# Routing of the early groups on VectorE, with small operands in PSUM

## The chip, the cores and the metric

The kernel runs on one core of one Trainium2 chip. The metric is the time of one execution in device microseconds (us). A core has a matrix engine (TensorE, PE in the profile), VectorE (DVE), ScalarE (ACT), GpSimd (POOL) and queues that issue DMA transfers (SyncE, SP). Each engine works through its own queue of instructions in order; semaphores hold an instruction until what it needs is there. SBUF is the on-chip memory, 128 partitions wide; PSUM is the smaller memory into which TensorE writes its products.

## The reference

Linear attention over 8 batches of 8 heads with 576 rows, then a mixture of 8 experts over the 4608 rows that come out of it. Each row goes to one expert only.

```python
def phi(x):
    proj = np.einsum('bhsd,df->bhsf', x, w_phi)
    proj = proj - np.max(np.abs(proj), axis=-1, keepdims=True)
    return np.concatenate([np.exp(proj), np.exp(-proj)], axis=-1)
q_p, k_p = (phi(q), phi(k))
kv = np.einsum('bhsf,bhsd->bhfd', k_p, v)
...
num = np.einsum('bhsf,bhfd->bhsd', q_p, kv)
...
logits = x @ w_gate
expert_idx = np.argmax(logits, axis=1)
logits_shift = logits - logits.max(-1, keepdims=True)
probs = np.exp(logits_shift)
probs /= probs.sum(-1, keepdims=True) + 1e-09
gate_w = probs[np.arange(N), expert_idx]
...
    h = np.maximum(xe @ w1[e], 0.0)
    ye = h @ w2[e]
    out[mask] = gate_w[mask, None] * ye
```

## The kernel before

**Two parts.** Up to about 424 us the attention runs; then the routed rows are gathered expert by expert, in blocks of 128, and go through the two products of their expert, mostly two blocks at a time. All products are made from pairs of rounded operands: a tile x is split into a high part (xh, kh, vh, wh: a copy in the rounded type, mostly on ScalarE) and the remainder (xl, kl, vl, wl: a subtraction, on VectorE or GpSimd), and three products take the place of one.

**Units.** The attention is worked in 16 units u = 0 to 15, about 24 us each: group g = u // 4 is two batches, and each of its four units is two heads. A unit projects its rows of k and q (`project`, L245 to 266: ps_proj on TensorE; mx, the row's maximum, and t, the subtraction, on VectorE), forms exponentials (e for k on ScalarE, then kh and kl; for q TensorE transposes t into pt and ScalarE makes qp), sums k against v into pk (L334), copies that to kvT (ScalarE, L351), unfolds it into pf and kf (L360, L370), and multiplies by qp into pn (L382). `normalize` (L404ff) divides (rec, xrow, lgc). lgc holds the logits of the group's rows, head by head. Rows of the result (xrow) are stored to DRAM for the gathers of the second part.

**Routing.** `route` (L590ff) is called once for each group. For groups 0 to 2 its steps are spread into the second, third and fourth unit of the next group, that is from u = 5, 9 and 13 on ("group 1", "2", "3" in the prediction are these three stretches, at about 130 to 156, 231 to 257 and 333 to 359 us): `spread` puts one step behind every sixth item of the unit. All 9 chunks of 128 rows are handled at once. The steps: lg (sum of the logits over the heads), lmax, the shift by it, cand (which expert has the maximum, as a number), choice (the smallest such), oh_b (one-hot, bf16), onehot (its float copy), gsum and base (running counts), some empty steps, prk (the rank of each row within its expert: nine products of oh_b on TensorE, all in one buffer), rks, rki (rank), rkb and rki (rank divided by 128, and the remainder), blk and rkr (their float copies), sel_p and sel_h (selection matrices by rkr, nine each, on VectorE and GpSimd), and the gates: ex on ScalarE, se (sum, plus 1e-9, reciprocal) and gt (the gate columns, stored to DRAM). Instructions named X in the code run on GpSimd for these groups and on VectorE for the last one. After the last early group `lead` (L734ff) finds the largest expert so far (lcand, ld, key, before), its rows (bl, b0, pl, gidx0) and gathers them early. The last group is routed at about 430 us in two parts, at the start of the expert part, and `place` (L552ff) lays out the blocks (first, paired, start, spot).

**What sets the order.** The products on TensorE follow a written order (`half` and `ordered`: sums into pk, unfolding and pn interleaved). Everything else is placed by a scheduler that goes by data and priorities; a block under `tc.high_priority(offset=200)` is taken earlier. Each engine then runs its list in the order found. PSUM buffers come from pools with two buffers for each tag: ps_pr for ps_proj, ps_tr for pt, ps_nm for pn, and ps_kv with the one tag "pk", which pk, pf, prk, pc, pl and pp share.

Of the kernel before, what the change touches and what calls it, by code (L numbers as in the profile page):

```python
# [19 lines left out]
P = 128  # L20
# [3 lines left out]
E = 8  # L24
# [4 lines left out]
NC = 9  # L29
# [9 lines left out]
NEARLY = (NG - 1) * NC  # L39
# [10 lines left out]
def tile_linear_attention_moe(  # L50
# [11 lines left out]
    nc = tc.nc  # L62
# [101 lines left out]
    blk = rt.tile([P, NTILE], F32, name="blk")  # L164
# [429 lines left out]
    def route(g, lgc, c0, n, final=None):  # L594
# [9 lines left out]
        def tile_of(name, shape, dtype=F32, **kw):  # L604
            r[name] = sg.tile(shape, dtype, name=name, **kw)[:, 0:n]
            return r[name]
# [20 lines left out]
        def first_top():  # L627
            V.tensor_reduce(choice[:, js], r["cand"], axis=AX.X, op=ALU.min)

        def one_hot():  # L630
            oh_b = tile_of("oh_b", [P, NC, E], BF16)
            V.tensor_tensor(
                oh_b,
                iota_em.unsqueeze(1).to_broadcast([P, n, E]),
                choice[:, js].unsqueeze(2).to_broadcast([P, n, E]),
                op=ALU.is_equal,
            )
            X.tensor_copy(onehot[:, js, :], oh_b)
            r["base_b"] = sg.tile([P, E], BF16, name="base_b")
            X.tensor_copy(r["base_b"], base)  # L640
# [9 lines left out]
        def sum_up():  # L650
            if not final:
                gsum = sg.tile([P, E], F32, name="gsum")
                V.tensor_reduce(gsum, onehot[:, js, :].rearrange("p c e -> p e c"), axis=AX.X, op=ALU.add)
                X.tensor_tensor(base, base, gsum, op=ALU.add)

        def count_ranks():
            oh_b, base_b = r["oh_b"], r["base_b"]
            prk = ps_kv.tile([P, n, E], F32, name="prk", tag="pk")
            T.matmul(prk, ltri, oh_b, start=True, stop=False)
            for c in range(n - 1):  # L660
                m = n - 1 - c
                T.matmul(
                    prk[:, c + 1 :, :], ones, oh_b[:, c : c + 1, :].to_broadcast([P, m, E]), start=False, stop=False
                )
            T.matmul(prk, ones, base_b.unsqueeze(1).to_broadcast([P, n, E]), start=False, stop=True)
            with tc.high_priority(offset=200 if final is None else 0):
                V.tensor_tensor(tile_of("rks", [P, NC, E]), prk, onehot[:, js, :], op=ALU.mult)

        def rank():
            with nc.allow_low_precision("ranks are integers"):  # L670
                V.tensor_reduce(tile_of("rki", [P, NC], I32), r["rks"], axis=AX.X, op=ALU.add)

        def rank_parts():
            rkb = tile_of("rkb", [P, NC], I32)
            V.tensor_single_scalar(rkb, r["rki"], 7, op=ALU.arith_shift_right)
            V.tensor_single_scalar(r["rki"], r["rki"], P - 1, op=ALU.bitwise_and)

        def rank_values():
            X.tensor_copy(blk[:, js], r["rkb"])
            X.tensor_copy(tile_of("rkr", [P, NC], bufs=2), r["rki"])  # L680

        def select_a(c):

# [15 lines left out]
            A.activation(tile_of("ex", [P, NC, E]), r["lg"], AF.Exp)  # L699

        def gate_sum():
            V.tensor_reduce(tile_of("se", [P, NC]), r["ex"], axis=AX.X, op=ALU.add)
            X.tensor_scalar_add(r["se"], r["se"], 1e-9)

        def gate_store():
            V.reciprocal(r["se"], r["se"])
# [1 line left out]
            X.tensor_copy(gt[:, 0:n], r["se"].unsqueeze(2).to_broadcast([P, n, XW - DM]))  # L708
            store_rows(g, gt, DM, XW - DM, c0, n)

        steps = [logits, top, shift, candidates, first_top, one_hot]
        selects = [lambda c=c: select(c) for c in range(n)]
        ranks = [rank, rank_parts, rank_values]
        gates = [gate, gate_sum, gate_store]
        if final is not None:

            def all_of(fs):
# [7 lines left out]
                *selects,  # L725
                all_of(gates),
            ]
        return steps + [sum_up] + PAUSE * [pause] + [count_ranks, pause] + ranks + selects + gates


    ON_ACT = (0, 2, 4, 6, 8)
# [2 lines left out]
    def lead():  # L734


        r = {}

        def pick():
            base_b = sg.tile([P, E], BF16, name="lbase_b")  # L740
            V.tensor_copy(base_b, base)
            r["base_b"] = base_b

        def pick_lead():
            pc = ps_kv.tile([P, E], F32, name="pc", tag="pk")
            T.matmul(pc, ones, r["base_b"], start=True, stop=True)
            top = sg.tile([P, 1], F32, name="top")
            V.tensor_reduce(top, pc, axis=AX.X, op=ALU.max)
            cand = sg.tile([P, E], F32, name="lcand")
            V.tensor_scalar(cand, pc, top, -float(E), op0=ALU.is_ge, op1=ALU.mult)  # L750
            V.tensor_tensor(cand, cand, iota_e, op=ALU.add)
            ld = sg.tile([P, 1], F32, name="ld")
            V.tensor_reduce(ld, cand, axis=AX.X, op=ALU.min)
            V.tensor_scalar_add(lead_e, ld[0:1], float(E))
            key = sg.tile([P, E], F32, name="key")
            V.tensor_scalar(key, iota_em, ld, -2.0 * E, op0=ALU.is_equal, op1=ALU.mult)
            V.tensor_tensor(key, key, iota_e, op=ALU.add)

            V.tensor_tensor(
                before,  # L760
                key.unsqueeze(2).to_broadcast([P, E, E]),
                key.unsqueeze(1).to_broadcast([P, E, E]),
                op=ALU.is_gt,
            )
            r["ld"] = ld

        def find():
            bl = sg.tile([P, NEARLY], F32, name="bl")
            V.tensor_scalar(bl, choice[:, 0:NEARLY], r["ld"], 64.0, op0=ALU.not_equal, op1=ALU.mult)
            V.tensor_tensor(bl, bl, blk[:, 0:NEARLY], op=ALU.add)  # L770
            b0 = sg.tile([P, NEARLY, NLEAD], BF16, name="b0")
            V.tensor_tensor(
                b0,
                iota_p[:, 0:NLEAD].unsqueeze(1).to_broadcast([P, NEARLY, NLEAD]),
                bl.unsqueeze(2).to_broadcast([P, NEARLY, NLEAD]),
                op=ALU.is_equal,
            )
# [470 lines left out]
```

## Time and profile before

| what | value |
|---|---|
| median of 3 runs | 932.68 us (931.11 to 932.99) |
| the profiled execution | 931.82 us |
| its span, first to last instruction | 929.9 us (1.92 around it) |
| mean granted TensorE clock | 0.99 |
| TensorE busy | 895.1 us, 96% of the span |
| VectorE busy | 589.4 us, 63% |
| ScalarE busy | 592.4 us, 64% |
| GpSimd busy | 496.6 us, 53% |

TensorE is busy nearly all the time and the other engines for little more than half of it. Such a share is a mean over stages, so the views by stretch and the list of TensorE's waits tell more than these numbers.

### The profile page before, as it was taken

What the parts mean: (1) busy time and instruction counts of PE and PEld (TensorE: products, weight loads), DVE (VectorE), ACT (ScalarE), POOL (GpSimd) and SP (SyncE); (2) the same over time, 40 slices, a digit from 0 to 9 for tenths busy, and PEclk for the clock granted to TensorE, in tenths of its full rate; (3) what the DMA queues carried; (4) which work ended last, traced back from release to release, by engine and by line L of the source; (5) the groups of instructions that cost most, each with busy time, mean ns of one, the idle gap of its engine ahead of it and who ended that gap; (6) DMA issues with size and microseconds to landing.
All of it is one profiled execution on the core that took longest, in us unless ns stands there. A gap on an engine that the chain in (4) does not pass through costs nothing. (4 is left out here: it accounts for less than half of the span.)

```text
span 929.9 us, 18409 instructions
## 1 busy us (share of the span) xinstructions
PE 895.1 (96%) x6831; PEld 837.6 (90%) x6831; DVE 589.4 (63%) x1015; ACT 592.4 (64%) x897; POOL 496.6 (53%) x356
## 2 busy tenths in 40 slices
PE   7999999999899999999799999999999999999995
PEld 6999989999899989999699999999999999987883
DVE  7777778777877778859844444444444444457850
ACT  6987766777688766656455555555555555568951
POOL 6766668666886669634533333333333333347641
PEclk9999999999999999999999999999999999999998
DMA  5233333333323333142143143431434634664100
GB/s 154 83 115 106 106 99 90 106 106 105 76 72 103 99 99 102 53 152 95 58 127 114 45 158 115 159 113 46 153 115 159 217 112 149 225 210 128 45 24 15
DMA packets 64620, 102.45 MB, mean 110 GB/s; under 512 B 10702, under 2 KB 28622, under 8 KB 64528
## 3 DMA queue, kind: packets, MB, share of 16 engines
q1 hardware_dynamic: 57136, 80.31, 28.1%
q0 software_dynamic: 6720, 20.80, 7.1%
q8 instruction: 54, 0.88, 0.4%
q14 instruction: 38, 0.31, 0.1%
q10 hardware_dynamic: 672, 0.15, 0.1%
HBM read 136.81 MB, written 20.26 MB: 169 GB/s over the span
## 5 line engine op out<-in xcount | busy, mean ns | idle before, releaser
L951 DVE TENSOR_TENSOR wl<-raw,wh 128x1024 fp32r<-128x1024 f32 x137 | 184.4, 1358 | 139.1 <-ACT wh L950 135.9
L950 ACT CAST wh<-raw 128x1024 fp32r<-128x1024 f32 x184 | 191.7, 1050 | 96.3 <-PE po L1015 68.3
L951 POOL TENSOR_TENSOR wl<-raw,wh 128x1024 fp32r<-128x1024 f32 x47 | 115.5, 2461 | 176.1 <-ACT wh L950 168.6
L993 PE MATMUL pm<-xh,wh 128*128 128x256 f32 x544 | 154.4, 284 | 0.7 <-ACT xh L975 0.7
L994 PE MATMUL pm<-xl,wh 128*128 128x256 f32 x544 | 154.8, 285 | 0.2 <-DVE xl L976 0.2
L382 PE MATMUL pn<-kf,qp 128*128 128x73 f32 x1024 | 154.8, 254 | 0.0
L995 PE MATMUL pm<-xh,wl 128*128 128x256 f32 x544 | 154.5, 284 | 0.0
L382 PEld LDWEIGHTS pn<-kf,qp 128*128 128x128 f32 x1024 | 148.7, 190 | 0.2
L259 DVE TENSOR_REDUCE mx<-ps_proj 128x4 f32<-128x512 f32 (+1 forms) x160 | 100.8, 630 | 62.5 <-PE ps_proj L255 61.9
L282 POOL TENSOR_TENSOR kl<-e,kh 128x1024 fp32r<-128x1024 f32 x47 | 112.1, 2385 | 39.1 <-ACT kh L280 39.1
L242 POOL TENSOR_TENSOR xl<-xr,xh 128x512 fp32r<-128x512 f32 (+2 forms) x63 | 88.2, 1402 | 46.4 <-ACT xh L241 46.0
L1014 PE MATMUL po<-wl,hh 128*128 128x512 f32 x272 | 106.7, 392 | 3.0 <-DVE wl L951 3.0
L1013 PE MATMUL po<-wh,hh 128*128 128x512 f32 x272 | 109.1, 401 | 0.0
L993 PEld LDWEIGHTS pm<-xh,wh 128*128 128x128 f32 x544 | 104.7, 193 | 3.3 <-ACT xh L975 0.9
L994 PEld LDWEIGHTS pm<-xl,wh 128*128 128x128 f32 x544 | 104.9, 193 | 2.8 <-DVE xl L976 0.4
L1015 PE MATMUL po<-wh,hl 128*128 128x512 f32 x272 | 106.0, 390 | 0.0
L995 PEld LDWEIGHTS pm<-xh,wl 128*128 128x128 f32 x544 | 104.9, 193 | 0.0
L260 DVE TENSOR_TENSOR t<-ps_proj,mx 128x512 f32<-128x512 f32 (+1 forms) x160 | 101.3, 633 | 3.8
L334 PE MATMUL pk<-kl,vh 128*65 128x256 f32 x320 | 97.2, 304 | 1.3 <-DVE kl L282 1.1
L334 PE MATMUL pk<-kh,vl 128*64 128x256 f32 x320 | 97.8, 306 | 0.0
L334 PE MATMUL pk<-kh,vh 128*65 128x256 f32 x320 | 97.7, 305 | 0.0
L253 PE MATMUL ps_proj<-w_hi,xh 128*128 128x256 f32 x288 | 92.0, 319 | 4.8 <-DVE t L260 4.6
(220 smaller groups left out, 2018.1 us busy)
## 6 DMA issues: line engine op xcount, KB each, us to landing
raw<-w SPq DMA_DIRECT2D x184, 512.0 KB
vt<-vv SPq DMA_DIRECT2D x15, 640.0 KB
x_dram<-xrow SPq DMA_DIRECT2D x30, 256.0 KB
xr<-kT SPq DMA_DIRECT2D x15, 320.0 KB
xr<-qT SPq DMA_DIRECT2D x15, 320.0 KB
xr<-kT SPq DMA_DIRECT2D x17, 256.0 KB
xr<-qT SPq DMA_DIRECT2D x17, 256.0 KB
x_dram<-xrow SPq DMA_DIRECT2D x32, 32.0 KB
```

The source lines that it names most:

```text
L260: V.tensor_tensor(t[:, 0 : 2 * n, :], psv, mx[:, 0 : 2 * n].unsqueeze(2).to_broadcast([P, 2 * n, F]), op=ALU.subtract,)
L282: eng.tensor_tensor(kl, e[:, 0:m], kh, op=ALU.subtract)
L334: return T.matmul(st["pk", bb][0:n, hh, :], (vl if j == 1 else vh)[:, 2 * (c + (bb if c == 8 else 0)) + hh, 0:n], (kl if j == 2 else kh)[: ...
L382: m = T.matmul(st["pn"][:, 2 * (c % 3) + hh, :], qp[:, s, s0 + hh, :] if c < 8 else qp[:, s, hh, bb : bb + 2].rearrange("p b q -> p (b q)" ...
L950: A.copy(th, raw[k])
L951: (G if k in (POOL_LO if u else POOL_LO0) else V).tensor_tensor(tl, raw[k], th, op=ALU.subtract)
L993: T.matmul(pm[:, i], th, xh[:, k, :], start=(k == 0), stop=False)
L994: T.matmul(pm[:, i], th, xl[:, k, :], start=False, stop=False)
L995: T.matmul(pm[:, i], tl, xh[:, k, :], start=False, stop=(k == KD - 1))
L1013: T.matmul(po, hh[:, i, r], th[:, c], start=(i == j == 0), stop=False)
L1014: T.matmul(po, hh[:, i, r], tl[:, c], start=False, stop=False)
L1015: T.matmul(po, hl[:, i, r], th[:, c], start=False, stop=(i == 1 and j == 3))
```

## The change

For the early groups the steps from lg to blk and rkr are on VectorE alone, and most of them read or write a small tile in PSUM, from the pool ps_kv: plm (the maxima, and the comparison with them), pch (the choice), prki (rank, its remainder and quotient), pse (the sum for the gate). Three steps (top, shift with candidates, first choice with one-hot) become two, `tops` and `pick`, each at high priority. GpSimd keeps onehot and base, gt, and sel_h. base_b is cast on ScalarE. gsum and rks read oh_b in place of onehot. The sum for the gates comes one empty step later. In `lead` pc, lcand and key share one PSUM tile (plead), key is copied to SBUF for the comparison of all pairs, and bl is in PSUM. For the last group rank and parts are one function and the comparison is as it was; the order of its instructions moves too. Line numbers behind L627 shift.

```diff
+        def tops():
+            pm = ps_kv.tile([P, NC, E + 1], F32, name="plm", tag="pk")
+            lmax = pm[:, 0:n, E : E + 1].to_broadcast([P, n, E])
+            with tc.high_priority(offset=200):
+                V.tensor_reduce(pm[:, 0:n, E], r["lg"], axis=AX.X, op=ALU.max)
+                V.tensor_tensor(pm[:, 0:n, 0:E], r["lg"], lmax, op=ALU.is_ge)
+                V.tensor_tensor(r["lg"], r["lg"], lmax, op=ALU.subtract)
+                V.tensor_tensor(
+                    tile_of("cand", [P, NC, E]),
+                    pm[:, 0:n, 0:E],
+                    iota_em.unsqueeze(1).to_broadcast([P, n, E]),
+                    op=ALU.mult,
+                )
+        def pick():
+            pch = ps_kv.tile([P, NC], F32, name="pch", tag="pk")[:, 0:n]
+            with tc.high_priority(offset=200):
+                V.tensor_reduce(pch, r["cand"], axis=AX.X, op=ALU.min)
+                V.tensor_tensor(
+                    tile_of("oh_b", [P, NC, E], BF16),
+                    iota_em.unsqueeze(1).to_broadcast([P, n, E]),
+                    pch.unsqueeze(2).to_broadcast([P, n, E]),
+                    op=ALU.is_equal,
+                )
+                V.tensor_copy(choice[:, js], pch)
+            G.tensor_copy(onehot[:, js, :], r["oh_b"])
+            r["base_b"] = sg.tile([P, E], BF16, name="base_b")
+            A.copy(r["base_b"], base)
...
-                V.tensor_reduce(gsum, onehot[:, js, :].rearrange("p c e -> p e c"), axis=AX.X, op=ALU.add)
+                V.tensor_reduce(gsum, r["oh_b"].rearrange("p c e -> p e c"), axis=AX.X, op=ALU.add)
...
-                V.tensor_tensor(tile_of("rks", [P, NC, E]), prk, onehot[:, js, :], op=ALU.mult)
+                V.tensor_tensor(tile_of("rks", [P, NC, E]), prk, oh_b, op=ALU.mult)
...
+                    pr = ps_kv.tile([P, 2, NC], I32, name="prki", tag="pk")[:, :, 0:n]
+                    with tc.high_priority(offset=200):
+                        V.tensor_reduce(pr[:, 0], r["rks"], axis=AX.X, op=ALU.add)
+                        V.tensor_single_scalar(pr[:, 1], pr[:, 0], P - 1, op=ALU.bitwise_and)
+                        V.tensor_single_scalar(pr[:, 0], pr[:, 0], 7, op=ALU.arith_shift_right)
+                        V.tensor_copy(blk[:, js], pr[:, 0])
+                        V.tensor_copy(tile_of("rkr", [P, NC], bufs=2), pr[:, 1])
+                    return
...
-            V.tensor_reduce(tile_of("se", [P, NC]), r["ex"], axis=AX.X, op=ALU.add)
-            X.tensor_scalar_add(r["se"], r["se"], 1e-9)
+                pse = ps_kv.tile([P, NC], F32, name="pse", tag="pk")[:, 0:n]
+                with tc.high_priority(offset=200):
+                    V.tensor_reduce(pse, r["ex"], axis=AX.X, op=ALU.add)
+                    V.tensor_scalar_add(r["se"], pse, 1e-9)
...
-        steps = [logits, top, shift, candidates, first_top, one_hot]
+        steps = [logits, top, shift, candidates, first_top, one_hot] if final is not None else [logits, tops, pick]
...
-        gates = [gate, gate_sum, gate_store]
+        gates = [gate, pause, gate_sum, gate_store]
...
-        return steps + [sum_up] + PAUSE * [pause] + [count_ranks, pause] + ranks + selects + gates
+        return steps + [sum_up] + PAUSE * [pause] + [count_ranks, pause, rank_parts] + selects + gates
...
-            pc = ps_kv.tile([P, E], F32, name="pc", tag="pk")
+            pl = ps_kv.tile([P, 3, E], F32, name="plead", tag="pk")
+            pc, cand, key = (pl[:, i] for i in range(3))
...
-            bl = sg.tile([P, NEARLY], F32, name="bl")
+            bl = ps_kv.tile([P, NEARLY], F32, name="bl", tag="pk")
```

Three places of the new order. The first is VectorE at the beginning of group 1's routing, before and then after (lines in the form: line, operation, result<-operands, shape).

```order
L609 TENSOR_REDUCE lg<-lgc 128x72
L259 TENSOR_REDUCE mx<-ps_proj 128x4
L617 TENSOR_REDUCE lmax<-lg 128x9
L260 TENSOR_TENSOR t<-ps_proj,mx 128x512
L259 TENSOR_REDUCE mx<-ps_proj 128x4
L628 TENSOR_REDUCE choice<-cand 128x9
L260 TENSOR_TENSOR t<-ps_proj,mx 128x512
L632 TENSOR_TENSOR oh_b<-iota_em,choice 128x72
L259 TENSOR_REDUCE mx<-ps_proj 128x4
L653 TENSOR_REDUCE gsum<-onehot 128x8
L260 TENSOR_TENSOR t<-ps_proj,mx 128x512
```

```order
L635 TENSOR_REDUCE plm<-lg 128x9
L260 TENSOR_TENSOR t<-ps_proj,mx 128x512
L636 TENSOR_TENSOR plm<-lg,plm 128x9x8
L259 TENSOR_REDUCE mx<-ps_proj 128x4
L637 TENSOR_TENSOR lg<-lg,plm 128x72
L638 TENSOR_TENSOR cand<-plm,iota_em 128x72
L260 TENSOR_TENSOR t<-ps_proj,mx 128x512
L648 TENSOR_REDUCE pch<-cand 128x9
L259 TENSOR_REDUCE mx<-ps_proj 128x4
L649 TENSOR_TENSOR oh_b<-iota_em,pch 128x72
L655 COPY choice<-pch 128x9
L683 TENSOR_REDUCE gsum<-oh_b 128x8
```

The comparison, the subtraction and the product have come in where the choice waited for GpSimd; oh_b, the copy of choice and gsum now stand in one piece ahead of a t.

The second is TensorE at the end of the sum pk of the same unit, before and after, with the engines that an instruction waits for (Activation is ScalarE; the number behind a name is its instance).

```order
L334 MATMUL pk_1883<-kl_1545,vh0_168 65x256
L382 MATMUL pn_2081<-kf_1917,qp_1655 128x73
L253 MATMUL ps_proj_2095<-w_hi_113,xh_1957 128x256 [waits DVE_49,PE_49]
L254 MATMUL ps_proj_2095<-w_lo_114,xh_1957 128x256
L255 MATMUL ps_proj_2095<-w_hi_113,xl_1958 128x256
L253 MATMUL ps_proj_2095<-w_hi_113,xh_1957 128x256
L254 MATMUL ps_proj_2095<-w_lo_114,xh_1957 128x256
L255 MATMUL ps_proj_2095<-w_hi_113,xl_1958 128x256
L334 MATMUL pk_2109<-kh_1891,vh1_171 65x256
L334 MATMUL pk_2109<-kh_1891,vl1_173 64x256
```

```order
L695 LDWEIGHTS ones_124
L695 MATMUL prk_2090<-base_b_1958,ones_124 128x72
L382 MATMUL pn_2083<-kf_1917,qp_1655 128x73
L334 MATMUL pk_2124<-kh_1891,vh1_171 65x256 [waits Activation_49]
L334 MATMUL pk_2124<-kh_1891,vl1_173 64x256
L334 MATMUL pk_2124<-kl_1892,vh1_171 65x256
L253 MATMUL ps_proj_2110<-w_hi_113,xh_1968 128x256 [waits DVE_49]
L254 MATMUL ps_proj_2110<-w_lo_114,xh_1968 128x256
```

The rank products (prk; eight rows of them stand above these) have moved ahead of the first product of the next pk, which now waits for ScalarE, where it waited for nothing.

The third is GpSimd in the same stretch, before and after.

```order
L282 TENSOR_TENSOR kl<-e,kh 128x1024
L242 TENSOR_TENSOR xl<-xr,xh 128x640
L310 TENSOR_TENSOR vl_170<-vt,vh_168 128x1280
L640 CAST base_b<-base 128x8
L679 CAST blk<-rkb 128x9
L242 TENSOR_TENSOR xl<-xr,xh 128x512
L680 CAST rkr<-rki 128x9
L694 TENSOR_SCALAR sel_h<-iota_pb,rkr,hbase 128x128 x4
L282 TENSOR_TENSOR kl<-e,kh 128x1024
L694 TENSOR_SCALAR sel_h<-iota_pb,rkr,hbase 128x128 x5
```

```order
L310 TENSOR_TENSOR vl_170<-vt,vh_168 128x1280
L242 TENSOR_TENSOR xl<-xr,xh 128x640
L282 TENSOR_TENSOR kl<-e,kh 128x1024
L242 TENSOR_TENSOR xl<-xr,xh 128x512
L734 TENSOR_SCALAR sel_h<-iota_pb,rkr,hbase 128x128 x6
L282 TENSOR_TENSOR kl<-e,kh 128x1024
L734 TENSOR_SCALAR sel_h<-iota_pb,rkr,hbase 128x128 x3
```

The additions and copies of the routing are gone from it, vl stands ahead of xl and kl where it stood behind them, and six sel_h stand ahead of a kl where four did.

## Rows read from the trace of the kernel before

**Rows 1.** The page, busy time, share of the span and instructions of TensorE.
```profile
PE 895.1 (96%) x6831; PEld 837.6 (90%) x6831; DVE 589.4 (63%) x1015; ACT 592.4 (64%) x897; POOL 496.6 (53%) x356
```

**Rows 2.** TensorE's waits, whole span: us in total, times, longest.
```profile
PE pt L291 <- DVE t L260: 10.2, 9, 1.6
```

**Rows 3.** Windows: length, then busy us of each engine, granted clock, DMA.
```profile
30.00:130.00 100.00, 100.00 (x938) 99.94 (x938) 72.59 (x149) 78.01 (x133) 65.09 (x34) 1.00 0.37 108
130.00:156.00 26.00, 22.42 (x200) 21.82 (x199) 21.31 (x50) 17.08 (x29) 21.39 (x22) 0.93 0.32 83
```

**Rows 4.** Timeline of TensorE, group 1: start, us, instruction [idle before <-releaser].
```profile
133.74 0.36 PE L253 MATMUL ps_proj<-w_hi,xh 128*128 128x256 f32 x1 [0.61 <-DVE t L260]
...
136.70 1.09 PE L291 MATMUL pt<-ident,t 128*128 128x128 f32 x4 [1.43 <-DVE t L260]
...
149.80 0.66 PE L291 MATMUL pt<-ident,t 128*128 128x128 f32 x4 [1.54 <-DVE t L260]
```

**Rows 5.** Timeline of VectorE, the same stretch.
```profile
132.77 0.23 DVE L628 TENSOR_REDUCE choice<-cand 128x9 f32<-128x72 f32 x1 [1.45 <-POOL cand L625]
...
133.51 1.65 DVE L632 TENSOR_TENSOR oh_b<-iota_em,choice 128x72 bf16<-128x72 f32 x1
...
145.68 0.23 DVE L667 TENSOR_TENSOR rks<-prk,onehot 128x72 f32<-128x72 f32 x1 [1.07 <-PE prk L665]
...
146.82 2.34 DVE L675 TENSOR_SCALAR rkb<-rki 128x9 int32<-128x9 int32 x1
...
149.74 0.93 DVE L676 TENSOR_SCALAR rki<-rki 128x9 int32<-128x9 int32 x1
```

**Rows 6.** Timeline of GpSimd, the same stretch.
```profile
132.39 0.34 POOL L625 TENSOR_TENSOR cand<-cand,iota_p 128x72 f32<-128x72 f32 x1
132.69 2.38 POOL L282 TENSOR_TENSOR kl<-e,kh 128x1024 fp32r<-128x1024 f32 x1
...
144.93 1.56 POOL L242 TENSOR_TENSOR xl<-xr,xh 128x640 fp32r<-128x640 f32 x1
146.44 2.68 POOL L310 TENSOR_TENSOR vl<-vt,vh 128x1280 fp32r<-128x1280 f32 x1
...
154.41 2.39 POOL L282 TENSOR_TENSOR kl<-e,kh 128x1024 fp32r<-128x1024 f32 x1
```

**Rows 7.** Two lines, all their instructions: ns shortest/median/longest, first and last start.
```profile
L632 DVE TENSOR_TENSOR oh_b<-iota_em,choice x5: 174/1648/1652, 133.5 to 431.6; 128x72 bf16<-128x72 f32 x3, 128x48 bf16<-128x48 f32 x1, 128x24 bf16<-128x24 f32 x1
```
```profile
L675 DVE TENSOR_SCALAR rkb<-rki x5: 166/1994/2340, 146.8 to 433.7; 128x9 int32<-128x9 int32 x3, 128x6 int32<-128x6 int32 x1, 128x3 int32<-128x3 int32 x1
```

**Rows 8.** The same of rec, which reads PSUM and writes SBUF.
```profile
L409 DVE TENSOR_SCALAR rec<-pn x48: 146/165/167, 37.7 to 425.8; 128x6 f32<-128x6 f32 x48
```

**Rows 9.** Timeline of ScalarE, group 1.
```profile
140.97 0.58 ACT L351 COPY kvT<-pk 65x512 f32<-65x512 f32 x1 [1.03 <-PE pk L334]
...
143.03 1.26 ACT L309 CAST vh<-vt 128x1280 fp32r<-128x1280 f32 x1
```

**Rows 10.** Timeline of VectorE, group 3.
```profile
348.43 0.49 DVE L741 CAST lbase_b<-base 128x8 bf16<-128x8 f32 x1
```

**Rows 11.** Windows in group 1; the granted clock is the third number from the end.
```profile
136.00:138.00 2.00, 1.30 (x7) 1.33 (x7) 2.00 (x5) 0.52 (x2) 1.89 (x3) 0.67 0.00 0
138.00:140.00 2.00, 2.00 (x12) 2.00 (x11) 1.56 (x3) 1.94 (x4) 1.14 (x1) 0.50 0.46 130
```

**Rows 12.** Timelines of VectorE and TensorE at the lead.
```profile
380.73 2.42 DVE L769 TENSOR_SCALAR bl<-choice,ld 128x27 f32<-128x27 f32 x1
```
```profile
384.58 0.39 PE L253 MATMUL ps_proj<-w_hi,xh 128*128 128x256 f32 x1 [0.46 <-DVE t L260]
```

**Rows 13.** Timelines of VectorE, GpSimd and TensorE at the start of the expert part.
```profile
441.37 4.25 DVE L951 TENSOR_TENSOR wl<-raw,wh 128x1024 fp32r<-128x1024 f32 x1
```
```profile
441.21 1.03 POOL L914 TENSOR_TENSOR eg<-eg,iota_p 1x344 f32<-1x344 f32 x1
```
```profile
445.68 0.50 PE L1014 MATMUL po<-wl,hh 128*128 128x512 f32 x1 [3.01 <-DVE wl L951]
```

More of the change, by code (lines that the diff above doesn't have):

```diff
@@ L666, in count_ranks, with rank_parts @@
             with tc.high_priority(offset=200 if final is None else 0):
-                V.tensor_tensor(tile_of("rks", [P, NC, E]), prk, onehot[:, js, :], op=ALU.mult)
-        def rank():
+                V.tensor_tensor(tile_of("rks", [P, NC, E]), prk, oh_b, op=ALU.mult)
+        def rank_parts():
             with nc.allow_low_precision("ranks are integers"):
[L671 to L676, printed above, removed]
+                if final is None:
+                    pr = ps_kv.tile([P, 2, NC], I32, name="prki", tag="pk")[:, :, 0:n]
[6 more added lines that the diff above has]
+                    return
+                rki = tile_of("rki", [P, NC], I32)
+                V.tensor_reduce(rki, r["rks"], axis=AX.X, op=ALU.add)
+                V.tensor_single_scalar(tile_of("rkb", [P, NC], I32), rki, 7, op=ALU.arith_shift_right)
+                V.tensor_single_scalar(rki, rki, P - 1, op=ALU.bitwise_and)
         def rank_values():
-            X.tensor_copy(blk[:, js], r["rkb"])
-            X.tensor_copy(tile_of("rkr", [P, NC], bufs=2), r["rki"])
+            if final is not None:
+                V.tensor_copy(blk[:, js], r["rkb"])
+                V.tensor_copy(tile_of("rkr", [P, NC], bufs=2), r["rki"])
         def select_a(c):
@@ L701, in gate_sum @@
         def gate_sum():
-            V.tensor_reduce(tile_of("se", [P, NC]), r["ex"], axis=AX.X, op=ALU.add)
-            X.tensor_scalar_add(r["se"], r["se"], 1e-9)
+            tile_of("se", [P, NC])
+            if final is None:
+                pse = ps_kv.tile([P, NC], F32, name="pse", tag="pk")[:, 0:n]
+                with tc.high_priority(offset=200):
+                    V.tensor_reduce(pse, r["ex"], axis=AX.X, op=ALU.add)
+                    V.tensor_scalar_add(r["se"], pse, 1e-9)
+            else:
+                V.tensor_reduce(r["se"], r["ex"], axis=AX.X, op=ALU.add)
+                V.tensor_scalar_add(r["se"], r["se"], 1e-9)
         def gate_store():
@@ L709, in gate_store @@
             store_rows(g, gt, DM, XW - DM, c0, n)
-        steps = [logits, top, shift, candidates, first_top, one_hot]
+        steps = [logits, top, shift, candidates, first_top, one_hot] if final is not None else [logits, tops, pick]
         selects = [lambda c=c: select(c) for c in range(n)]
-        ranks = [rank, rank_parts, rank_values]
-        gates = [gate, gate_sum, gate_store]
+        ranks = [rank_parts, rank_values]
+        gates = [gate, pause, gate_sum, gate_store]
         if final is not None:
@@ L748, in pick_lead @@
             V.tensor_reduce(top, pc, axis=AX.X, op=ALU.max)
-            cand = sg.tile([P, E], F32, name="lcand")
             V.tensor_scalar(cand, pc, top, -float(E), op0=ALU.is_ge, op1=ALU.mult)
@@ L754, in pick_lead @@
             V.tensor_scalar_add(lead_e, ld[0:1], float(E))
-            key = sg.tile([P, E], F32, name="key")
             V.tensor_scalar(key, iota_em, ld, -2.0 * E, op0=ALU.is_equal, op1=ALU.mult)
             V.tensor_tensor(key, key, iota_e, op=ALU.add)
+            keys = sg.tile([P, E], F32, name="key")
+            V.tensor_copy(keys, key)
             V.tensor_tensor(
@@ L761, in pick_lead @@
                 key.unsqueeze(2).to_broadcast([P, E, E]),
-                key.unsqueeze(1).to_broadcast([P, E, E]),
+                keys.unsqueeze(1).to_broadcast([P, E, E]),
                 op=ALU.is_gt,
```

## The prediction

> **What bounds the kernel now.** I read the page first: TensorE is busy for 895.1 of 929.9 us [rows 1], so only time in which it waits, or runs at a low clock, can be won. The list of TensorE's waits comes next: its largest entry is the transposes pt waiting for VectorE's t, 10.2 us in nine waits [rows 2]. The windows then say where: in 30 to 130 us TensorE is busy without a gap, while in the 26 us in which group 1 is routed it is busy for 22.42 [rows 3]. The stretches of groups 2 and 3 read alike, which is where the nine waits come from. So 3.6 us are idle in each of three stretches, 10.8 in all, and nearly nothing in the units between. The timeline of group 1 gives the three waits: 0.61 before ps_proj, 1.43 and 1.54 before pt, each ended by t on VectorE [rows 4].
>
> Why t is late is read beside it on VectorE [rows 5] and GpSimd [rows 6]. The first t stands behind choice, which waited 1.45 for GpSimd's second cand, and that cand stood behind an xl. The second t stands behind oh_b, which took 1.65 and ends at 135.16, just as GpSimd's kl ends (132.69 + 2.38 = 135.07). The third stands behind rkb, which took 2.34 and ends as GpSimd's vl does (149.12). The same two lines take 0.174 and 0.166 in the final routing, where GpSimd is idle [rows 7]. So an instruction of 0.2 us is held for as long as GpSimd's instruction lasts. Not everything is held: rks, which reads one operand from PSUM, took 0.23 at 145.68 [rows 5], in the middle of an xl on GpSimd (144.93 to 146.49, [rows 6]). Of the Trainium skill, "SBUF — State Buffer", section Who interferes with whom, states this as a lock on a shared pair of ports, taken by whoever issues first, and exempts VectorE instructions with at most one SBUF input outside the two-port modes; the trace agrees in oh_b, rkb and rks.
>
> **The change, part by part, for one early group.**
>
> *VectorE, taken away.* The idle 1.45 before choice goes, as no step of the choice is on GpSimd any more. oh_b, rkb and rki take 4.92 together [rows 5]; with their inputs in PSUM I give each 0.23, the price of rks, so 4.2 go.
>
> *VectorE, added.* Seven small instructions: the comparison, the subtraction, the product, the copies of choice, blk and rkr, and the addition to se. Between 0.17 (rkb's shortest, [rows 7]) and 0.23 (rks) each makes 1.2 to 1.6; I take 1.4. They end with less on VectorE: 1.45 + 4.2 - 1.4 = 4.2 us earlier. The copies blk and rkr read PSUM, so I count them as not held; were they, each could cost what rki costs, 0.93 [rows 5]. The Trainium skill's "Perfetto Trace Analysis", section Optimizing Scalar/DVE Operations, speaks against this part: it gives VectorE some 60 ns of overhead on SBUF and 125 on PSUM, and by it 13 instructions on PSUM would cost an estimated 0.85 us more per group. The row that bears on it is rec, which reads PSUM and takes 0.165 [rows 8], no more than rkb on SBUF when it is alone. I keep the rows.
>
> *TensorE.* 4.2 us are more than the 3.6 it loses, so I followed the new order from instruction to instruction on the old time base, to see what is late next. The t's before the first ps_proj and pt come 0.7 to 1 us ahead of need. The third is ready within about 0.1 of it. Two new things are near. First, the nine rank products now stand straight behind the last product of the old pk, and the next pk behind them; both PSUM buffers of that tag are then held, by prk and by the old pk, and the next pk waits until ScalarE has copied the old one out (kvT, 0.58 [rows 9]). Six or eight small products cover part: I take 0.4, with 0.2 to 0.6 as ends (a whole kvT). Second, GpSimd: vl is now ahead of both xl and kl, and six sel_h ahead of the kl that today starts at 154.41 [rows 6]. By my walk this kl ends about when TensorE wants it; I take a wait of 0.3, with 0 and 1.0 as ends. Left are 0.7 us per group, and 3.6 - 0.7 = 2.9 are won: **8.7 us** for three. Moving gate_sum a unit later costs nothing: the gate columns are read hundreds of us later.
>
> *Group 3's extra cast.* lbase_b still reads SBUF alone. It took 0.49 [rows 10] and lands elsewhere; rkb shows what a bad place costs, 2.34 [rows 5]. I take 0.5, from 0 to 2.2: **-0.5**.
>
> *Clock.* Right after the waits of 0.61 and 1.43 in group 1 the granted clock falls: 0.67 in 136 to 138 us and 0.50 (the lower level, 1.2 GHz) in 138 to 140 [rows 11]. TensorE's busy 1.30 and 2.00 us there would have taken 0.87 and 1.00 at 2.4 GHz: 1.4 us lost. Groups 2 and 3 wait as long and keep their clock, so this is a marginal fall, and I expect it gone with the waits: **+1.4**, or 0 if it stays.
>
> *The lead* (which expert is the largest, after group 3). bl took 2.42 beside a kl on GpSimd, and TensorE then waited 0.46 [rows 12]. With bl and key in PSUM that wait goes: **+0.5**. What follows, the gathers, is not waited for.
>
> *The start of the MoE part.* The final routing keeps its instructions, but the order around it moves: on VectorE the weight residue wl of piece 5 goes from before first to behind spot, the hl of the second block later too. Today the wl of piece 6 takes 4.25, behind GpSimd's eg and wl, and TensorE waits 3.01 for it [rows 13]. In the new order two wl stand there together. Piece 5 escapes if it issues before eg; then piece 6 follows before or behind GpSimd's wl. If both escape, 3.0 are won; if piece 5 is held as well, TensorE stops for it first, up to half of today's wait again, 1.5, since GpSimd's list there does not grow. I take 0, from +3.0 to -1.5.
>
> **Sum.** 8.7 - 0.5 + 1.4 + 0.5 = 10.1 us off. The profiled execution took 931.82 (929.9 in the span, 1.92 around it), 0.86 below the median of 932.68: 921.7 by the one, 922.6 by the other. I say **922.0**.
>
> **Rivals.**
> (a) *Half of it is given back.* VectorE stays tight in these stretches and the two new waits come at their upper ends: 0.6 + 1.0 for 0.7 is 0.9 more per group, 2.7 in all, and with the clock's fall kept (1.4) and a bad place for the cast (1.0) the time is 927. For it: VectorE's slack is 0.3 us or less at four points of my walk. Against: it loses 4.2 us of work for TensorE's 3.6.
> (b) *The MoE start is freed too.* Both wl escape: 3.0 more, 919.0; with the other terms at their good ends, 917. For it: on VectorE the first of the two wl stands a step earlier relative to eg. Against: GpSimd's eg and wl wait for little else and may still come first.
> (c) *Slower: GpSimd becomes late for TensorE.* vl is now ahead of xl and kl in GpSimd's queue and waits for ScalarE's vh. In today's trace vh starts at 143.03 and lasts 1.26 [rows 9], so it ends at 144.29; my walk has it at about 139.0, because the new order puts it right behind kvT. Should it stay where it is, the whole queue of GpSimd runs 5.3 us later than in my walk in each group, and TensorE waits for that at the xl and kl behind. The gain is used up from 10.1 / 3 = 3.4 us of lateness on. Time: 931.8 - 10.1 + 3 x 5.3 = 937.6. Against: vh has no data to wait for but an early load and a free buffer.
> (d) *It does not do what it says*: VectorE is held also with one operand in PSUM. Then the held instructions stay, the seven added ones are held in part, and the waits remain: 932 to 933, no change. Against: rks at 0.23 [rows 5].
>
> **Chances.** The forecast (919.5 to 924.5) 0.55; (a) to 928 0.21; (b) 0.12; (d) 0.04; (c) 0.08. The range is 917.5 to 928.0: it leaves out (c), (d) and the lower half of (b). A difference of 0.2%, 1.9 us, is about what a measurement of this kernel can tell from none. Faster by more: 0.55 + 0.21 + 0.12 = 0.88; within it 0.04; slower 0.08.
>
> **What would show it.** In the new profile oh_b, the ranks' shift and mask and bl should take 0.15 to 0.25 each, whatever GpSimd runs; waits of pt for t should fall from 10.2 us to about 2; TensorE should be busy for some 25 of 26 us in the three stretches, and the clock at 1.00 in the first. A wait of the next pk for ScalarE's kvT of 0.2 to 0.6 should be new, and perhaps one for GpSimd's kl. I am wrong if the idle time returns there under another name, above all as pk or ps_proj waiting for GpSimd (c), or if oh_b still takes 1.6 us (d); the wait of po for wl tells (b).

## The result

The changed kernel takes 923.72 us (median; 922.39 to 925.29), the kernel before 932.46 beside it. The ratio is 0.9914 (95% interval 0.9900 to 0.9928): 8 us, or 0.9%, faster by the ratio; the two medians are 8.7 apart. The forecast of 922.0 (917.5 to 928.0) holds the time. The profiled execution of the changed kernel took 922.39, with a span of 920.5.

The list of TensorE's waits of the changed kernel, whole span, to be read beside [rows 2] (columns: who waited for whom, us in total, times, longest):

```profile
PE pn L382 <- DVE kf L370: 4.4, 3, 1.5
PE po L1062 <- DVE wl L999: 2.3, 1, 2.3
PE ps_proj L253 <- DVE t L260: 2.2, 2, 1.2
PE pt L291 <- DVE t L260: 1.5, 5, 0.7
```

The largest entry of before, pt for t with 10.2 us, is down to 1.5. A new one is the largest: pn waits for kf three times, once in each routing stretch.

The windows over the three stretches and over the lead (length, busy us of TensorE first, granted clock third from the end), beside [rows 3] and [rows 11]:

```profile
128.00:156.00 28.00, 26.21 (x249) 25.62 (x247) 25.95 (x62) 19.22 (x34) 23.49 (x19) 1.00 0.31 91
229.00:257.00 28.00, 26.21 (x248) 25.63 (x247) 25.95 (x64) 19.71 (x36) 24.12 (x19) 1.00 0.29 88
329.00:359.00 30.00, 28.24 (x267) 27.62 (x266) 28.41 (x69) 21.58 (x38) 24.93 (x20) 1.00 0.28 83
359.00:400.00 41.00, 41.00 (x431) 40.95 (x430) 28.72 (x71) 29.84 (x51) 27.50 (x17) 1.00 0.36 100
```

TensorE now idles 1.8 us per stretch, where it was 3.6 (24.42 of 28 us busy in 128 to 156 before); the clock of group 1 stays at 1.00; the stretch of the lead has no idle time.

What became of the instructions that were held, by line (ns shortest/median/longest), beside [rows 7]:

```profile
L649 DVE TENSOR_TENSOR oh_b<-iota_em,pch x3: 219/221/222, 133.3 to 333.6; 128x72 bf16<-128x72 f32 x3
```
```profile
L707 DVE TENSOR_SCALAR prki<-prki x3: 164/164/165, 142.1 to 342.4; 128x9 int32<-128x9 int32 x3
```

oh_b fell from 1.65 to 0.22 us, the ranks' mask from 0.93 to 0.16, and all three groups agree within a few ns: these instructions are not held by GpSimd any more.

And where the new wait comes from. The timelines of VectorE, GpSimd and TensorE at the end of group 1's stretch:

```profile
151.69 2.75 DVE L282 TENSOR_TENSOR kl<-e,kh 128x512 fp32r<-128x512 f32 x1
154.36 0.68 DVE L259 TENSOR_REDUCE mx<-ps_proj 128x4 f32<-128x512 f32 x1
154.96 0.45 DVE L370 COPY kf<-pf 128x292 f32<-128x292 f32 x1
```
```profile
146.78 4.75 POOL L734 TENSOR_SCALAR sel_h<-iota_pb,rkr,hbase 128x128 bf16<-128x128 bf16 x6
151.51 2.38 POOL L282 TENSOR_TENSOR kl<-e,kh 128x1024 fp32r<-128x1024 f32 x1
```
```profile
151.74 0.44 PE L291 MATMUL pt<-ident,t 128*128 128x128 f32 x2 [0.16 <-DVE t L260]
...
155.46 0.44 PE L382 MATMUL pn<-kf,qp 128*128 128x73 f32 x2 [1.50 <-DVE kf L370]
```

Of the 1.8 us, the timeline shows 1.50 before pn and 0.16 before a pt. Another 0.13, too short for the list of waits, stands before the next pk, which starts as ScalarE's copy of the old pk (kvT) ends:

```profile
137.15 0.58 ACT L351 COPY kvT<-pk 65x512 f32<-65x512 f32 x1
```
```profile
137.24 0.41 PE L382 MATMUL pn<-kf,qp 128*128 128x73 f32 x2
137.78 0.33 PE L334 MATMUL pk<-kh,vh 128*65 128x256 f32 x1
```

A kl of 512 columns, which VectorE does in 0.68 when nothing holds it (e2 has such a one at 152.25 us), starts 0.18 us behind a GpSimd kl and lasts until 154.4, half a microsecond after that has ended. mx and kf stand behind it, and pn behind kf. GpSimd's kl is the one that six sel_h now stand ahead of. In the kernel before the same two met as well, but at the tail: GpSimd's kl began at 154.41 [rows 6], VectorE's 1.9 us later, and VectorE lost 0.4 us by it. Timeline of VectorE before:

```profile
156.28 1.08 DVE L282 TENSOR_TENSOR kl<-e,kh 128x512 fp32r<-128x512 f32 x1
```

The change brings VectorE to this place 4.6 us earlier (151.69) and GpSimd only 2.9 (151.51), and so they meet in full.

Where the 9.4 us between the two profiled executions went, by the distance between the same instructions (lg of each group, cni at the last routing, gidx, the end): group 1 3.3 us, of which 1.8 are idle time of TensorE and 1.4 the clock; group 2 1.8; group 3 and the lead 3.3, of which idle time explains 2.7 (1.9 and 0.8); the start of the expert part 0.3 up to gidx; the rest, 0.9, behind it, where the clock fell in the profile of before and not in this one. Some 0.6 in the third piece is not accounted for.

### The profile page after: what moved, and what is told of

It is laid out like the page before. It is cut to its first block, busy times and chain, and to the rows that moved or that the text cites. A ratio compares the mean times of both kernels' runs of the same rounds, so it can differ in the third digit from the quotient of the medians.

```text
span 920.5 us, 18442 instructions
## 1 busy us (share of the span) xinstructions
PE 892.2 (97%) x6831; PEld 834.6 (91%) x6831; DVE 586.1 (64%) x1037; ACT 592.4 (64%) x900; POOL 491.6 (53%) x335
## 5 line engine op out<-in xcount | busy, mean ns | idle before, releaser
L1111 POOL DMA_INDIRECT out<-ob,sidx x41 | 46.4, 1131 | 91.4 <-ACT ob L1109 85.5
```

## The experiments

Two theories. **Held**: a VectorE instruction whose operands lie in SBUF alone is held by the GpSimd instruction that runs beside it, and an operand in PSUM frees it. **Steps**: the gain comes from taking the steps off GpSimd's queue, wherever the operands lie. Held, as it is put here, is too wide: not every instruction on SBUF alone is held. In the kernel before, the sum rki (SBUF alone) took 0.23 in the middle of the xl of 144.93 to 146.49 [rows 6], a reciprocal (rec) 0.19 at 154.83 beside GpSimd's kl, and nine sel_p ran unheld beside GpSimd's sel_h, while in the changed kernel two sel_p beside a kl and an xl took 2.50. Before, and then after:

```profile
145.94 0.23 DVE L671 TENSOR_REDUCE rki<-rks 128x9 int32<-128x72 f32 x1
...
151.38 2.15 DVE L694 TENSOR_SCALAR sel_p<-iota_pb,rkr,part 128x128 bf16<-128x128 bf16 x9
```
```profile
144.34 2.50 DVE L734 TENSOR_SCALAR sel_p<-iota_pb,rkr,part 128x128 bf16<-128x128 bf16 x2
```

So even in the changed kernel instructions of the routing are held, but no wait of TensorE followed from these two. Why sums, reciprocals and what runs beside sel_h go free, no run here asks.

Later runs ask what holds kf, and what the lead and the start of the expert part are worth. All ratios are to the kernel before on the same chip.

| run | edit | us | ratio (95%) |
|---|---|---|---|
| e1_sbuf | the change with SBUF tiles | 951.42 | 1.021 (1.0133 to 1.0287) |
| e2_psum_alone | before, with PSUM tiles | 934.43 | 1.0026 (1.0012 to 1.004) |
| e3_old_lead | the change, old lead | 929.5 | 0.9978 (0.9966 to 0.999) |
| e4_kl8_gpsimd | the change, three kl moved | 919.75 | 0.9865 (0.9848 to 0.9883) |
| e5_wl7_vector | the change, one wl moved | 922.75 | 0.9902 (0.9879 to 0.9926) |
| e6_choice_only | the change, old ranks | 927.09 | 0.9948 (0.9929 to 0.9966) |
| e7_both | e4 and e5 together | 921.23 | 0.9887 (0.9863 to 0.9911) |
| e8_new_lead | before, new lead | 930.35 | 0.9984 (0.9968 to 1.0) |
| e9_five_sel | the change, selections a step later | 920.95 | 0.989 (0.9871 to 0.9908) |
| e10_after_again | the change | 923.55 | 0.992 (0.99 to 0.9939) |
| e11_kl8_again | as e4 | 921.68 | 0.9896 (0.9878 to 0.9915) |

### e1: the same instructions, operands in SBUF

```diff
-            pm = ps_kv.tile([P, NC, E + 1], F32, name="plm", tag="pk")
...
+            cd = tile_of("cand", [P, NC, E])
+            lm = tile_of("lmax", [P, NC])
...
-            pch = ps_kv.tile([P, NC], F32, name="pch", tag="pk")[:, 0:n]
+            pch = sg.tile([P, NC], F32, name="se")[:, 0:n]
...
-                    pr = ps_kv.tile([P, 2, NC], I32, name="prki", tag="pk")[:, :, 0:n]
+                    pr = [sg.tile([P, NC], I32, name=x)[:, 0:n] for x in ("rkb", "rki")]
...
-                pse = ps_kv.tile([P, NC], F32, name="pse", tag="pk")[:, 0:n]
+                pse = r["se"]
```

> The changed kernel with the four small tiles of the early groups' routing (maxima and comparison, choice, rank parts, gate sum) in SBUF instead of PSUM; the same instructions on the same engines. Theory (VectorE is held by GpSimd when it reads and writes SBUF only): the shift and mask of the ranks and oh_b take 0.9 to 2.4 us again where GpSimd runs beside, t is late again, and at least 6 of the 8.7 us won are lost: 929 to 936 us. Rival (the gain comes from taking the steps off GpSimd's queue, where the operands lie does not matter): 923 to 925 us, oh_b at 0.2.

Measured 951.42, further out than the 929 to 936 expected. The four executions lie between 944.96 and 960.68, so the size is known only roughly: 21 to 37 us more than the change's median (measured on another chip), and even the shortest is 10 us above the slowest of the 19 executions of the kernel before beside it (934.84). The choice is called se in this trace, since pch takes a tile of that name. VectorE's groups of instructions by line (count, busy us, mean ns of one) and TensorE's first two waits:

```profile
L708 DVE TENSOR_SCALAR rki<-rkb 128x9 int32<-128x9 int32 x3 | 6.9, 2309 | 0.0
L638 DVE TENSOR_TENSOR lg<-lg,lmax 128x72 f32<-128x72 f32 x3 | 5.4, 1797 | 0.0
L639 DVE TENSOR_TENSOR cand<-cand,iota_em 128x72 f32<-128x72 f32 x3 | 4.7, 1566 | 0.0
L637 DVE TENSOR_TENSOR cand<-lg,lmax 128x72 f32<-128x72 f32 x3 | 3.9, 1298 | 0.0
```
```profile
PE ps_proj L253 <- DVE se L649: 10.1, 3, 3.4
PE pt L291 <- DVE t L260: 6.0, 5, 1.7
```

Four instructions of 0.16 to 0.23 us take 1.3 to 2.3 each. The comparison of group 1 shows it most plainly, as it stands beside the same xl of GpSimd in both kernels (from 130.78 in the change, from 130.70 here). The change, then e1:

```profile
130.85 0.23 DVE L636 TENSOR_TENSOR plm<-lg,plm 128x72 f32<-128x72 f32 x1
```
```profile
130.79 1.29 DVE L637 TENSOR_TENSOR cand<-lg,lmax 128x72 f32<-128x72 f32 x1
```

Two that were expected to be held were not: oh_b took 0.22 and the ranks' shift 0.17 on average. GpSimd stood idle when oh_b of group 1 ran (137.15; its next instruction starts at 137.43), and so it did for the shift (146.26, between a kl and a sel_h). The clock falls in all three stretches as well:

```profile
130.00:156.00 26.00, 20.97 (x174) 20.50 (x173) 21.85 (x50) 15.82 (x26) 17.29 (x17) 0.87 0.12 34
```

TensorE is busy for 20.97 of 26 us there, and granted 0.87. The scheduler put some of the later instructions in another order, so not every microsecond is the holding's own; but the durations leave no doubt. Steps falls: without the PSUM tiles the same move off GpSimd is a loss of 1.3 to 2.9%.

### e2: the operands in PSUM, the steps left on GpSimd

```diff
+                r["pch"] = ps_kv.tile([P, NC], F32, name="pch", tag="pk")[:, 0:n]
...
+                    V.tensor_reduce(r["pch"], r["cand"], axis=AX.X, op=ALU.min)
...
+                    pr = ps_kv.tile([P, 2, NC], I32, name="prki", tag="pk")[:, :, 0:n]
...
+                        V.tensor_copy(blk[:, js], pr[:, 0])
+                        V.tensor_copy(tile_of("rkr", [P, NC], bufs=2), pr[:, 1])
```

> The kernel before with PSUM operands alone: choice and the rank parts in PSUM tiles (with their copies to blk and rkr on VectorE, at high priority), while the shift and both cand steps, se and base stay on GpSimd, and the lead is as before. Theory: oh_b and the rank parts fall to 0.15 to 0.25, two of three waits per stretch (1.43 and 1.54) go, the wait of choice for GpSimd's cand (1.45) and the ps_proj wait of 0.6 stay: 924 to 928 us. Rival (the GpSimd steps are what costs): 930 to 933 us.

Measured 934.43, 0.26% slower than before: outside the theory's range and the rival's. The theory's durations were right (the rank parts take 0.17):

```profile
L640 DVE TENSOR_TENSOR oh_b<-iota_em,pch 128x72 bf16<-128x72 f32 x3 | 0.7, 220 | 0.0
```

But rkr is ready earlier, the sel_h are issued earlier, and eight of them now stand ahead of an xl, the ninth, and the kl that TensorE wants. GpSimd and TensorE in group 1's stretch:

```profile
147.72 6.66 POOL L713 TENSOR_SCALAR sel_h<-iota_pb,rkr,hbase 128x128 bf16<-128x128 bf16 x8
...
156.37 2.34 POOL L282 TENSOR_TENSOR kl<-e,kh 128x1024 fp32r<-128x1024 f32 x1
```
```profile
133.66 0.36 PE L253 MATMUL ps_proj<-w_hi,xh 128*128 128x256 f32 x1 [0.62 <-DVE oh_b L640]
136.25 0.63 PE L291 MATMUL pt<-ident,t 128*128 128x128 f32 x4 [0.88 <-DVE t L260]
158.77 0.34 PE L334 MATMUL pk<-kl,vh 128*65 128x256 f32 x1 [2.45 <-POOL kl L282]
```

The third wait is gone and one of 2.45 has come, for GpSimd: 3.95 us in place of 3.58. Group 2 reads alike. This is rival (c) of the prediction, GpSimd late for TensorE, in another kernel and by another queue order (sel_h, not vl). In group 3 no such wait came (1.5 us of waits in all); a loss stands behind it, where the old lead, which this run keeps, is now late for its products pl:

```profile
382.48 0.16 PE L803 MATMUL pl<-b,sel_p 128*128 128x3 bf16 x1 [1.96 <-DVE b L791]
```

So the PSUM operands of choice and ranks alone were no gain in this order: freeing VectorE shows only when what comes next, on GpSimd or in the lead, doesn't stand in the way. How much they would win with the new lead this run doesn't tell.

### e3 and e8: the lead, taken out of the change and put into the kernel before

In e3 key, cand and bl are SBUF tiles as before; in e8 the new lead is the only edit.

> The changed kernel with the lead as before (key, cand and bl in SBUF). Theory: bl and key are held by GpSimd again (1 to 2.5 us) and TensorE waits 0.5 to 0.8 once: 924.2 to 924.6 us. Rival (what was won there was hidden): 923.7 us, no wait in TensorE's list between 360 and 400 us.

> The kernel before with the lead of the changed one (plead and bl in PSUM), nothing else. In the changed kernel the old lead cost 5.8 us. Theory (the price of the held instructions of the lead depends on where TensorE's products pl stand; in the order of before only 0.5 to 0.7 us of waits are ended by them): 0.3 to 1 us less than before, ratio 0.999 to 1.000. Rival (the lead is worth its 5.8 us in either kernel): ratio 0.994.

In e8 the lead wins 0.16%, 1.5 us by the ratio; the interval, 0 to 3 us, ends at no change, holds the theory and leaves out the rival's 0.994. In e3 the old lead costs 0.6%, 5.8 us against the change's median, some ten times as much as expected. VectorE and TensorE of e3:

```profile
372.79 1.35 DVE L803 TENSOR_SCALAR key<-iota_em,ld 128x8 f32<-128x8 f32 x1
374.06 1.32 DVE L816 TENSOR_SCALAR bl<-choice,ld 128x27 f32<-128x27 f32 x1
375.30 2.37 DVE L804 TENSOR_TENSOR key<-key,iota_p 128x8 f32<-128x8 f32 x1
```
```profile
378.36 0.16 PE L831 MATMUL pl<-b,sel_p 128*128 128x3 bf16 x1 [3.43 <-DVE b L819]
```
```profile
359.00:400.00 41.00, 37.57 (x368) 37.30 (x367) 31.20 (x65) 26.13 (x45) 22.35 (x14) 0.92 0.26 74
```

In the order of the change the products pl stand some 9 us earlier, counted from the lg of group 3, where three held instructions in a row end 3.4 us too late for them, and the clock falls behind the stall (0.92 over 41 us, by an estimate from the 37.57 busy us about 3 more). In the order of before pl comes 4 us behind b, and the held instructions only made t late, by 0.46 and 0.2. An edit that is worth little in the old kernel was needed in the new one.

### e4, e9 and e11: what kf waits for

```diff
-        eng = G if c0 in (4, 6) or (c0 == 0 and st["u"] > 0) else V
+        eng = G if c0 in (4, 6) or (c0 == 0 and st["u"] > 0) or (c0 == 8 and st["u"] in (6, 10, 14)) else V
```

That is e4 and e11. In e9 the kl stay where they are, and one empty step stands ahead of the selections, which leaves five sel_h ahead of GpSimd's kl; on VectorE only the places of two sel_p move.

```diff
-        return steps + [sum_up] + PAUSE * [pause] + [count_ranks, pause, rank_parts] + selects + gates
+        return steps + [sum_up] + PAUSE * [pause] + [count_ranks, pause, rank_parts] + 1 * [pause] + selects + gates
```

> The changed kernel with the kl of piece 8 (128x512) of units 6, 10 and 14 on GpSimd instead of VectorE, where it takes 2.75 us beside a GpSimd kl and kf stands behind it. Theory (the new wait of pn for kf, 1.5 us in each of three stretches, is this one held instruction): the three waits go and the time is 919 to 920 us. Rival (VectorE is simply full there): only the 0.7 us of its own length are won each time, waits of 0.7 to 0.8 remain, 921.5 us. Second rival (GpSimd is then too late with its own kl): new waits of pk for kl, 923 us or more.

> The changed kernel with the selections one step later, so that five instead of six sel_h (0.79 us each) stand ahead of GpSimd's kl. Theory (kf waits for VectorE's kl of piece 8, which waits for exactly that GpSimd kl): GpSimd's kl ends 0.8 us earlier, VectorE's kl falls from 2.75 to about 1.95, the three waits of pn for kf from 1.5 to about 0.7, and the time by 2 to 2.4 us against the changed kernel. Rival (VectorE is full): no change in the waits.

> The changed kernel itself, beside the next run on the same chip: ratio to before 0.990 to 0.993.

> The kernel with kl of piece 8 of units 6, 10 and 14 on GpSimd again, beside the changed kernel on the same chip. If the 4 us between 923.72 and 919.75 are its own and not the chip's: 3 to 4.5 us below the changed kernel here. Otherwise within 2 us of it.

e10, the change again, came out at 0.992, as expected. e9 tells what kf waits for. GpSimd, VectorE, and TensorE's wait:

```profile
150.62 2.37 POOL L282 TENSOR_TENSOR kl<-e,kh 128x1024 fp32r<-128x1024 f32 x1
```
```profile
151.56 2.00 DVE L282 TENSOR_TENSOR kl<-e,kh 128x512 fp32r<-128x512 f32 x1
```
```profile
PE pn L382 <- DVE kf L370: 2.5, 3, 0.9
```

GpSimd's kl starts 0.9 us earlier, VectorE's lasts 2.00 in place of 2.75 (2.17 in groups 2 and 3), the three waits shrink from 4.4 to 2.5 in all, and the time falls by 2.6 us against the change on the same chip, a little more than the waits; no execution of either overlaps (920.85 to 921.09, 923.08 to 924.40). VectorE has the same instructions as in the change, so that it is full there is ruled out. That a VectorE instruction with two SBUF inputs collides with a GpSimd one that reads SBUF is what the Trainium skill states ("SBUF — State Buffer", section Who interferes with whom); here that is 2.75, 2.00 and 0.68 us for the same kl, by how much of GpSimd's kl is left. In e4 and e11 the waits of pn for kf are gone altogether. The time was 919.75 on one chip and 921.68 on another, where the change beside it took 923.55: 1.9 us won, fewer than the 3 to 4.5 that the edit was to have if the 4 us of e4 were its own. So part of those 4 us came with the chip. The time of e11 is also that of e4's rival (921.5); it is the waits, gone and not halved, that speak against it. A part comes back: in one of the three groups (the first in e4, the second in e11) another kl of VectorE, of 1024 columns, is now held instead. VectorE and TensorE of e4:

```profile
160.92 3.27 DVE L282 TENSOR_TENSOR kl<-e,kh 128x1024 fp32r<-128x1024 f32 x1
```
```profile
164.93 0.36 PE L253 MATMUL ps_proj<-w_hi,xh 128*128 128x256 f32 x1 [1.18 <-DVE rec L409]
```

e9 and e4 both beat the change and the kernel before; which of the two is faster the runs don't tell (0.989 and 0.9896 on one chip).

### e6: the choice alone

The ranks are as before (rki and rkb in SBUF, blk and rkr copied on GpSimd), the rest as in the change.

> The changed kernel with the ranks as before: rki and rkb in SBUF, the copies to blk and rkr on GpSimd; the choice (PSUM, VectorE alone), the gates and the lead stay changed. Theory: rkb and rki are held again (2 and 0.9 us in place of 0.16 each), one wait of pt for t of about 1.5 us per stretch is back: 926 to 929 us. The granted clock in group 1 stays at 1.00, since its fall came behind the two waits of the choice. Rival (the choice alone carries the gain): 923 to 924.5 us.

927.09, some 3 us slower than the change, as expected, but not in the way expected. In groups 1 and 2 rkb and rki are held (1.14 and 1.80 us), the pt wait of 1.5 is back, and the pn wait for kf of 1.5 is gone: with the ranks late, all nine sel_h stand ahead of the xl and kl, and no GpSimd kl meets VectorE's. So there the ranks' PSUM tiles won nothing on balance. The loss is in group 3 and behind it: a wait of pt of 2.2 and one of pn for kf of 0.9, and a fall of the clock behind the first.

```profile
348.90 1.12 PE L291 MATMUL pt<-ident,t 128*128 128x128 f32 x4 [2.20 <-DVE t L260]
```
```profile
348.00:352.00 4.00, 3.10 (x16) 3.10 (x17) 3.35 (x14) 1.09 (x2) 4.00 (x6) 0.61 0.03 10
```

Ahead of that t VectorE did rkb (1.14) and then a copy of base for the final routing, which this order has set beside a kl of GpSimd; in the change it takes 0.17, at 349.51:

```profile
344.97 2.35 DVE L670 CAST base_b<-base 128x8 bf16<-128x8 f32 x1
```

So most of that loss is another SBUF instruction in a bad place, and not the ranks themselves; what the ranks' tiles are worth alone this run leaves open.

### e5 and e7: the wait at the start of the expert part

```diff
-    POOL_LO0, POOL_LO = (1, 3, 7), (3, 7)
+    POOL_LO0, POOL_LO = (1, 3), (3, 7)
```

> The changed kernel with the first weight residue wl of piece 7 on VectorE instead of GpSimd. Theory (the one wait of po for wl at the start of the expert part, 2.3 us, is piece 6's wl held by GpSimd's eg and by its wl of piece 7, 4.27 us for 1.2): wl of piece 6 falls to about 2 us or less, the wait falls by at least 1.5 us, and the time is 921 to 922.2 us. Rival (the wait is hidden behind the gather: VectorE now does one wl more ahead of bsel, so the first gather comes 1.2 us later): the wait of px for the gather grows by what po wins, 923.5 to 924.5 us.

> The changed kernel with both edits: kl of piece 8 of units 6, 10, 14 on GpSimd, and the first wl of piece 7 on VectorE. If the two waits are independent, it has the 919.75 of the first edit alone less what the second alone wins (1.5 to 2.3): 917.5 to 918.3 us. Rival (the second is hidden): 919 to 920 us.

In e5 the wait of po for wl, 2.3 us, is gone, and wl of piece 6 takes 1.95 instead of 4.27. TensorE's list has instead:

```profile
PE px L1021 <- DMA xg<-x_dram,gidx: 2.2, 1, 2.2
```

It was 0.9 in the change. The gather starts 1.4 us earlier, but TensorE is there 2.7 earlier; and the clock of 424 to 462 us was 0.96 in this profile and 1.00 in the change's. The ratio, 0.9902, can't be told from the change's 0.9914 or 0.992, and e7 can't be told from e4. Counted from cni, TensorE begins px 1.2 us earlier than in the change: of the 2.3 won at po, about half comes back as waiting for the gather. The time, 922.75, lies between the theory's range and the rival's, and 921.23 of e7 lies above both of its own, which went by e4's 919.75. So these runs show half of the wait hidden behind the gather, and don't tell whether the other half reaches the end.

## Why the prediction was right, point by point

- **That VectorE's instructions are freed**: right, shown by e1 and by the durations. They take 0.16 to 0.23; 0.23 was taken. The seven added ones cost 0.15 to 0.23 each, as assumed, and the copies from PSUM are not held. The Trainium skill ("Perfetto Trace Analysis", section Optimizing Scalar/DVE Operations) gives VectorE some 60 ns of overhead on SBUF and 125 on PSUM; no such difference shows here. The copies to blk and rkr take 0.157 and 0.158 us from PSUM, and in e1, unheld, 0.162 and 0.165 from SBUF.
- **2.9 us per group, 8.7 in all**: the mechanism right, the size too high. Measured 1.8, 1.8 and 1.9, 5.5 in all (by the windows). The step that failed is the term for what is left. I expected 0.7 from two new waits, of the next pk for kvT (0.4) and of TensorE for GpSimd's kl (0.3). The first is there with 0.13, the second is not. What is left is 1.79: 0.13 of pk, 0.16 of pt and 1.50 of pn for kf. So TensorE is busy for 24.2 of 26 us in each stretch, where I expected some 25. I had followed that very GpSimd kl, but only as something that TensorE waits for. That it would hold a VectorE instruction in its turn I did not ask; I had looked for held instructions only among those of the routing, and the kl of VectorE are everyday work with two operands in SBUF.
- **The nine waits of [rows 2]** I misread as three for each stretch. Each stretch has two waits of pt (3.0 us) and one of ps_proj (0.6); three waits of pt, 1.2 us together, lie elsewhere. The 3.6 of each stretch, from which I worked, is right. And of the two unheld rkb of the final routing [rows 7] one ran beside sel_h (at 433.72), not beside an idle GpSimd.
- **-0.5 for lbase_b**: it took 1.05 in its new place, inside the bounds, and no wait of TensorE followed: 0.
- **+1.4 for the clock**: there in the profile, which has 1.00 in group 1. But the fall is not tied to one place. It stood in group 3 and at the start of the expert part in e8, in group 3 in e6, and at the start of the expert part in the second profile of the change (0.96 in 424 to 462 us). As an estimate for one stretch it is fair, as a fixed gain it is not; that the fall stood in group 1 in the one profile I read is luck. Over all executions on record with a clock, the mean granted clock is 0.9895 for the kernel before (42) and 0.991 for the change (8): by an estimate from the 895.1 busy us some 1.4 us, near what I took, but single executions of the kernel before range from 0.984 to 0.996.
- **+0.5 for the lead**: 0.8 in the stretch of the lead; in the kernel before e8 has 1.5, with 0 to 3 as its interval. That the change needs it (5.8 in e3) I didn't see; I priced it in the order of before.
- **0 for the start of the expert part, from +3.0 to -1.5**: one of the two wl escaped (1.21) and one was held (4.27 for the same reason as in [rows 13]); the wait went from 3.01 to 2.29, +0.7 (of which 0.3 had arrived at gidx). Rival (b), both free, put 3.0 on it; in e5, where the wait of po is gone, 1.2 are left at px, and what of it reaches the end isn't told.
- The sum with these terms: 5.5 + 1.4 + 0.8 + 0.7 = 8.4, against 10.1 forecast and 8.7 between the medians (9.4 between the profiled executions, with another 0.9 of the clock behind gidx). The groups were 3.2 too high; the cast, the lead and the start of the expert part together were 1.5 too low. That these cancel by half is luck.
- **Rival (a)**, half given back, came nearest to what the groups did (1.1 us per group more than I left, where it had 0.9), by a wait that it didn't name. **(c)** was wrong here: vl started at 138.98, as in my walk. **(d)** was wrong: oh_b takes 0.22.

## What to carry to other kernels

When small VectorE instructions on SBUF take as long as the GpSimd instruction beside them, give them one operand in PSUM; their number matters less than where they read. Read from the trace which are held: here comparisons, products, shifts, masks and casts beside GpSimd's xl, kl, vl, eg or wl, but not sums and reciprocals, and hardly anything beside sel_h. Then look at every other VectorE instruction with two SBUF operands that the new order sets beside a long GpSimd one, not only at those that were changed: the hold moves on to it, and with few microseconds of slack a shift by one 0.8 us instruction decides. Price an edit in the new order: one that is worth some 1 us alone can be the condition for 6.

## What the runs showed of the hardware that was not expected

A held VectorE instruction does not always get in when the GpSimd instruction ends. In e4 the kl of 160.92 us was held through an xl (to 161.44), a small copy and the next xl (161.54 to 163.10), and in the change the wl of 4.27 us through an eg and a wl behind it. In the other two groups of e4 kl got in behind the xl, and GpSimd's copy was held in its turn (gt, 1.23 us in place of 0.22). In the change and in e9 the kl of 512 columns did get in behind GpSimd's kl, though a row of sel_h followed at once, and this row was then slower (0.89 to 0.92 for each sel_h in place of 0.79). And a fall of TensorE's clock follows a stall of 1.4 to 3.4 us in some executions and not in others of the same length: 1.4 in group 1 of before, not in groups 2 and 3, which wait the same, and in e8, with the same waits, in group 3.
